# Batch 0's first product in six single PSUM banks, batch 1's exps moved ahead, and the activation tables loaded by hand, in an attention and feed-forward kernel

## The chip, the cores and the metric

The kernel runs on one core of one Trainium2 chip. The metric is the device time of one execution in microseconds (us); lower is better. Times inside an execution are counted from the start of the profile's span.

## What is computed

For 8 batches, 8 heads, 576 tokens of 64 dimensions, 32 packed queries p per head, all in float32:

```python
p_packed = sm_attn(p, k, v)              # softmax attention of the 32 packed queries over the tokens
out      = sm_attn(q, p_packed, p_packed) # the tokens attend to the 32 packed results
x = out.transpose(0, 2, 1, 3).reshape(8 * 576, 512)
h = x @ w_in                             # 512 -> 2048
g = h * np.cos(h)
return g @ w_out                         # 2048 -> 512
```

## The kernel before

All matrix work is in bfloat16 with float32 sums in PSUM. Batches go one after another through stages; within a stage the steps of the next batch's attention are laid between the matmuls of the current one. The order on every engine is the order of the program text (`tc.manual_schedule()`); the framework only adds the semaphores. Engines are PE (matmul), ACT (ScalarE), DVE (`V`, VectorE), POOL (`G`, GpSimd, which also issues the loads of k, q, v and the weights) and SP (which issues DMA transposes and the stores of the output).

The steps of a batch b, with the names that the profile shows:

- `load`: k, q, v come through POOL's DMA queue, cast to bf16 (`kbf`, `qbf`, `vbf`). `permute_v` copies v to `vp` (on POOL, batch 0 on DVE).
- k and q are transposed to `kT`, `qT`, either by `xbar` (a DMA transpose on SP's queue) or by `pe_T` (24 PE transposes in three groups, each evacuated from PSUM by ACT or DVE).
- `s1`: scores of p against k in two PSUM tiles, and their Exp on ACT (`a`, with row sums). `recips`: reciprocals of the sums on DVE (`r`, `rs`). `a` is transposed to `a1T` by `a1_xbar` (SP) or by PE (`a1_pe`, `a1_one`).
- `pp`: the packed result, 24 small matmuls of `vp` by `a1T`, copied to `ppT`. `ppw(b, n)`: its product with a quarter of w_in, copied to `PPW`, so that h can be formed from attention weights without forming x.
- `s2`: scores of q against the packed keys, Exp on ACT (`a2u`). `sums2`: sums over the packed tokens by a matmul with ones, and Ln on ACT (`lns`). `normalise`: Exp of minus that on ACT, and on DVE the product (`a2n`).
- `h_mm(b, fc)` for 16 slices fc of 128 hidden channels: h in PSUM by four matmuls of 288 columns (L250), cosine as Sin of h + pi/2 on ACT (`cosT`, L254), product on DVE (`gT`, L257). After fc 7 and 15 POOL copies the last 64 tokens to `joint`, which holds those of two batches.
- the output: for chunks of 128 tokens, 16 matmuls of `gT` by w_out (L303) into a bank `ot`, copied to `osb` by DVE and ACT in turn, stored by SP. These matmuls are the filler: `set_filler(b)` opens batch b's (64, or 80 where a chunk of `joint` is included), `fill(n)` issues n of them. The last chunk of all has a function of its own (L289).

PSUM has eight banks: three pairs (`psa()`, pool psA, used in turn) and two single ones (`bank()`, tag `ot`). Exp and Ln come from one activation table, Sin from another; before the change Exp's is loaded by hand (L354, L431, L454, L489) and Sin's by the compiler, at the first Sin (L254).

The stages: the head (loads, batch 0's attention, batch 1's s1); h(0), with the rest of PPW(0), `pp(1)` and q1's transposes in between; from `s2(1)` batch 1's attention and h(1) with batch 0's output as filler (`slot(1)` is the loop of h(1)); the same for stage 2 with `s1(2)`, `s1(3)`, `pp(2)`, h(2) and batch 1's output; a loop for stages 3 to 7; the output of batch 7.

POOL's `gate` copies read one element of a transposed tile, so that POOL's later loads are not issued before that transpose is done.

Of the kernel before, what the change touches and what calls it, by code (L numbers as in the profile page):

```python
# [8 lines left out]
FP32 = mybir.dt.float32  # L9
# [6 lines left out]
def kernel(  # L16
# [20 lines left out]
    EXP_SET = "natural_log_exp_and_others"  # L37

# [11 lines left out]
    A = ctx.enter_context(tc.tile_pool(name="psA", bufs=3, space=PSUM))  # L50
    O = ctx.enter_context(tc.tile_pool(name="psO", bufs=2, space=PSUM))

    ctx.enter_context(tc.manual_schedule())
# [24 lines left out]
    def psa(dt=FP32):  # L78
        return A.tile([128, 2, 512 if dt == FP32 else 1024], dt, name="psA", tag="A")

# [13 lines left out]
    def pe_T(n, b, engs=(V, V, V), groups=(0, 1, 2), own=False):  # L94
# [4 lines left out]
        for i in groups:  # L99
            ps = bank(BF16) if own else psa(BF16)[:, 0, :]  # L100
# [53 lines left out]
    def a1_pe(b, ys=(0, 1), own=False):  # L154
# [3 lines left out]
        for y in ys:  # L158
            ps = bank(BF16) if own else psa(BF16)[:, 0, :]
# [105 lines left out]
    n_out = [0]  # L265
# [29 lines left out]
    def out_gen(b):  # L295
        groups = [(0, 1), (2,), (3,)] if b == 0 else [(c,) for c in range(n_chunks(b))]
        for grp in groups:
            pss = {c: O.tile([128, DM], FP32, name="ot", tag="ot") for c in grp}
            for f0 in range(0, NFC, 4):
                for c in grp:  # L300
                    for fc in range(f0, f0 + 4):
# [41 lines left out]
    nc.sync.dma_start(out=p_raw[:, 0:2, :], in_=p_rows[:, 0:2, :])  # L343
# [5 lines left out]
    G.dma_start(out=p_raw[:, 2:4, :], in_=p_rows[:, 2:4, :])  # L349
# [12 lines left out]
    dup_p(0, 2, V)  # L362
    pack_p(0, 1)
# [186 lines left out]
```

## Time and profile before

| | |
|---|---|
| time, median of 3 runs | 254.32 us (254.19 to 255.27) |
| span of the profiled execution, first to last instruction | 252.3 us |
| granted TensorE clock, mean | 0.997 |
| PE, DVE, ACT, POOL busy | 92%, 65%, 68%, 23% |
| head, 0 to 22.7 us | first h matmul at 22.73 |
| h(0), 22.7 to 38.5 us | 15.8 us |
| stage 1, 38.5 to 63.9 us | 25.4 us |
| stage 2, 63.9 to 98.4 us | 34.5 us |
| stages 3, 4, 5, 6 | 25.5, 28.4, 26.1, 29.0 us |
| stage 7 and the last output | 21.9 and 23.0 us |

The profiled execution has no time of its own beside its span; it lies 2.0 us under the median of the timed runs, which counts what lies before the first and after the last instruction too. A line of the timeline gives start, length, engine, source line, operation, output and inputs, shapes and count, and in brackets how long the engine sat idle before it and what ended that. A PE line's length contains the pipeline's tail; two starts give the pace.

### The profile page before, as it was taken

To read this page: it belongs to the slowest core of one execution; us is meant where nothing else is said; L and a number is where in the kernel's file an instruction comes from. 1 tells how busy PE (TensorE), PEld (TensorE's weight loads), DVE (VectorE), ACT (ScalarE), POOL (GpSimd) and SP (SyncE) were. 2 spreads that over 40 slices of the span, in tenths; PEclk is the share of its full clock that TensorE was granted. 3 is DMA by queue.
4 is the path that set the end of the run, shared out by engine and by line. 5 is a ranking of instruction groups with operands and counts; after the bars stand their busy time and mean duration, and the time that the engine had idled before them with its cause. 6 is when DMAs were issued, how large, how long until landed. Compare 5 with 4: busy or idle time off the path is not lost.

```text
span 252.3 us, 4989 instructions
## 1 busy us (share of the span) xinstructions
PE 233.3 (92%) x1981; PEld 130.7 (52%) x2014; DVE 163.0 (65%) x245; ACT 170.5 (68%) x285; POOL 58.4 (23%) x71
## 2 busy tenths in 40 slices
PE   8786888999969999999999998999899999999993
PEld 3453463566435554465446553565356554665452
DVE  2548996789376977477847675479556874876110
ACT  2366888857558788878886667887877585873000
POOL 8442604200362243104313105020500000000000
PEclk9999999999999999999999999999999999999998
DMA  6999999999999989999999994979471112112133
GB/s 91 202 211 205 205 207 226 200 186 149 191 208 198 176 175 212 220 204 164 225 173 181 180 182 99 175 141 196 97 144 44 42 44 70 36 34 62 50 83 83
DMA packets 65270, 37.67 MB, mean 149 GB/s; under 512 B 37872, under 2 KB 60656, under 8 KB 65248
## 3 DMA queue, kind: packets, MB, share of 16 engines
q0 software_dynamic: 23184, 18.81, 48.8%
q1 hardware_dynamic: 41904, 18.42, 36.8%
q8 instruction: 15, 0.25, 0.4%
q10 hardware_dynamic: 160, 0.13, 0.2%
q14 instruction: 7, 0.06, 0.1%
HBM read 37.22 MB, written 9.44 MB: 185 GB/s over the span
## 4 chain that ended last, share of the span: by engine, by line
PE 74%; DVE 8%; ACT 7%; DMA 5%; issue 2%; POOL 2%; DVEq 0%; POOLq 0%; ACTq 0%
PE ot L303 42%; PE psA L250 22%; DMA w_in_bf<-in_moe_w_in_dram 5%; DVE gT L257 5%; PE psA L201 3%; ACT cosT L254 3%; PE psA L177 2%; PE psA L227 1%; PE ot L289 1%; ACT a2u L219 1%; ACT L489 1%; DVE rs L147 1%; PE psA L128 1%; DVE osb L76 1%; DVE PPW L76 1%
## 5 line engine op out<-in xcount | busy, mean ns | idle before, releaser
L303 PE MATMUL ot<-w_out_bf,gT 128*128 128x512 bf16 x483 | 126.9, 380 | 2.1 <-issue 1.3
L257 DVE TENSOR_TENSOR gT<-psA,cosT 128x576 bf16<-128x576 f32 x128 | 94.1, 754 | 31.1 <-ACT cosT L254 30.0
L254 ACT ACTIVATE cosT<-psA 128x576 bf16<-128x576 f32 x128 | 82.7, 652 | 29.8 <-PE psA L250 28.1
L250 PE MATMUL psA<-a2n,PPW 128*128 128x288 bf16 x512 | 84.0, 286 | 2.5 <-DVE PPW L76 1.0
L303 PEld LDWEIGHTS <-gT 128*128 128x128 bf16 x512 | 48.0, 98 | 42.6 <-issue 6.1
L250 PEld LDWEIGHTS <-PPW 128*128 128x128 bf16 x512 | 49.1, 98 | 36.5 <-issue 3.8
L76 DVE CAST PPW<-psA 128x1024 bf16<-128x1024 f32 (+1 forms) x23 | 25.8, 1128 | 12.1 <-PE psA L201 12.1
L261 POOL COPY joint<-gT 128x512 bf16<-128x512 bf16 x16 | 9.8, 614 | 88.7 <-DVE gT L257 88.7
L76 DVE COPY osb<-ot 128x512 f32<-128x512 f32 (+1 forms) x19 | 12.8, 671 | 16.9 <-PE ot L303 13.8
L74 ACT COPY osb<-ot 128x512 f32<-128x512 f32 (+1 forms) x18 | 10.3, 571 | 18.7 <-PE ot L303 14.1
L76 POOL COPY vp<-vbf 96x3072 bf16<-96x3072 bf16 x7 | 19.2, 2750 | 1.6 <-DMA vbf<-in_v_dram 1.6
L237 DVE SCALAR_TENSOR_TENSOR a2n<-a2u,r,lns 128x576 bf16<-128x576 bf16 x16 | 12.4, 813 | 9.6 <-ACT lns L235 9.6
L229 ACT ACTIVATE lns<-psA 128x576 f32<-128x576 f32 x16 | 10.3, 651 | 5.7 <-PE psA L227 5.3
L137 ACT ACTIVATE a<-psA 128x576 bf16<-128x576 f32 x16 | 10.2, 648 | 5.0 <-PE psA L128 5.0
L303 PE MATMUL ot<-w_out_bf,joint 128*128 128x512 bf16 x46 | 12.4, 380 | 0.1
L201 PE MATMUL psA<-w_in_bf,ppT 64*32 64x512 bf16 x224 | 10.4, 381 | 1.5 <-DVE gT L257 1.1
L219 ACT ACTIVATE a2u<-psA,rs 128x576 bf16<-128x576 f32 x16 | 11.0, 736 | 1.2 <-PE psA L128 1.1
L254 ACT ACT_TABLE_LOAD x8 | 10.3, 1283 | 0.1
L74 ACT CAST ppT<-psA 64x128 bf16<-64x128 f32 x24 | 6.2, 259 | 6.1 <-PE psA L103 2.9
L235 ACT ACTIVATE lns<-lns 128x576 f32<-128x576 f32 x16 | 10.0, 678 | 0.0
L341 PE MATMUL ot<-wz 128*128 128x512 bf16 x24 | 8.1, 472 | 1.5 <-DVE wz L353 1.2
L74 ACT CAST PPW<-psA 128x1024 bf16<-128x1024 f32 (+1 forms) x9 | 7.2, 826 | 2.6 <-PE psA L201 2.6
(71 smaller groups left out, 143.4 us busy)
## 6 DMA issues: line engine op xcount, KB each, us to landing
kbf<-in_k_dram POOLq DMA_DIRECT2D x8, 576.0 KB, 12.2
vbf<-in_v_dram POOLq DMA_DIRECT2D x8, 576.0 KB, 7.4
qbf<-in_q_dram POOLq DMA_DIRECT2D x8, 576.0 KB, 9.6
out_dram<-osb SPq DMA_DIRECT2D x24, 192.0 KB, 2.6
out_dram<-osb SPq DMA_DIRECT2D x22, 128.0 KB, 2.4
w_in_bf<-in_moe_w_in_dram POOLq DMA_DIRECT2D x4, 512.0 KB, 16.5
w_out_bf<-in_moe_w_out_dram POOLq DMA_DIRECT2D x4, 512.0 KB, 20.9
out_dram<-osb SPq DMA_DIRECT2D x26, 64.0 KB, 2.1
```

Of the source, the lines that this page charges most:

```text
L74: ACT.copy(out=out, in_=in_)
L76: eng.tensor_copy(out=out, in_=in_)
L137: ACT.activation(out=a1[b % 2][:, y, :, 0:TP].rearrange("p (e m) x -> p e m x", e=2), in_=ps[y][:, :, 0:HS].rearrange("p e (m x) -> p e m ...
L201: nc.tensor.matmul(ps[y][32 * x:32 * x + 32, :], ppT[b % 2][r, 2 * x + y, :], w_in_bf[r, x, n * 512:(n + 1) * 512], start=True, stop=True)
L219: ACT.activation(out=a2u[b][:, y].rearrange("p (e x) -> p e x", e=2), in_=ps[y][:, :, 0:HS], func=AF.Exp, scale=rs1[b][:, y:y + 1])
L229: ACT.activation(out=lns[b][:, y].rearrange("p (e x) -> p e x", e=2), in_=ps[:, :, 0:HS], func=AF.Ln)
L235: ACT.activation(out=lns[b][:, y], in_=lns[b][:, y], func=AF.Exp, scale=-1.0)
L237: V.scalar_tensor_tensor(out=a2n[b][:, y], in0=a2u[b][:, y], scalar=r1[b][:, y:y + 1], in1=lns[b][:, y], op0=ALU.mult, op1=ALU.mult)
L250: nc.tensor.matmul(ps[:, e, 0:HS], PPW[b][:, y, fc * 128:(fc + 1) * 128], a2n[b][:, y, e * HS:(e + 1) * HS], start=(y == 0), stop=(y == 1))
L254: ACT.activation(out=csv, in_=ps[:, :, 0:HS], func=AF.Sin, bias=PI_HALF)
L257: V.tensor_tensor(out=gT[b][:, fc, :].rearrange("p (e x) -> p e x", e=2), in0=ps[:, :, 0:HS], in1=csv, op=ALU.mult)
L303: nc.tensor.matmul(pss[c], w, w_out_bf[:, fc, :], start=(fc == 0), stop=(fc == NFC - 1))
```

## The change

- h(0) no longer uses `h_mm` but `h_one`: 512 tokens per slice in one bank, with the three pairs of psA closed and six single banks (psH) opened in their place for the time of h(0) (`banks(0)`, `banks(3)`). Two matmuls of 512 columns, a Sin and a product on 512. The last 64 tokens of all 16 slices follow at once in `h_rest(0)`, during h(1): 32 matmuls of 64 columns into one pair, one Sin and one product of 1024 columns, straight into `joint`.
- In the head p is loaded for two batches in one DMA on SP; k1's transposes go to the two `ot` banks between batch 0's sums; `s1(1)` comes right after `normalise(0)`, then Sin's table, then `ppw(0, 0)` whole, `a1_one(1)` and `recips(1)`.
- q1's transposes come after h(0) in single banks; batch 0's filler starts at `s2(1)`, with 18 matmuls before h(1) (4 were in h(0), 8 and 14 before h(1)).
- v2 is loaded ahead of q2 and k3; `permute_v(2)` and v3's load move into h(1); k2 is transposed by PE in h(1) (fc 7, 8, 9), q2 and k3 by SP from there; `load("k", 4)` follows `load("q", 3)`.
- `s1(3)`, `a1_xbar(3)` and `recips(3)` move from ahead of `pp(2)` to behind `normalise(2)`, which on SP is behind the transposes of q3 and k4; `permute_v(3)` stands ahead of the gate on k4.
- Both tables are loaded by hand: Sin's right behind the Exps, Exp's right behind the last Sin, ahead of the leftover filler. `osb` is copied by DVE between the Exps and by ACT during h (from h(1) on), no longer in turn.

```diff
--- before.py
+++ after.py
@@ -35,6 +35,7 @@
     EXP_SET = "natural_log_exp_and_others"
+    SIN_SET = "trig_and_small"
 
     const = ctx.enter_context(tc.tile_pool(name="const", bufs=1))
     bf_pool = ctx.enter_context(tc.tile_pool(name="bf", bufs=1))
@@ -47,10 +48,19 @@
     cos_pool = ctx.enter_context(tc.tile_pool(name="cos", bufs=3))
     o_pool = ctx.enter_context(tc.tile_pool(name="o", bufs=4))
     small = ctx.enter_context(tc.tile_pool(name="small", bufs=3))
-    A = ctx.enter_context(tc.tile_pool(name="psA", bufs=3, space=PSUM))
     O = ctx.enter_context(tc.tile_pool(name="psO", bufs=2, space=PSUM))
-
     ctx.enter_context(tc.manual_schedule())
+    psum = {"stack": ctx.enter_context(ExitStack())}
+
+    def banks(pairs):
+
+        psum["stack"].close()
+        if pairs:
+            psum["A"] = psum["stack"].enter_context(tc.tile_pool(name="psA", bufs=pairs, space=PSUM))
+        if pairs < 3:
+            psum["H"] = psum["stack"].enter_context(tc.tile_pool(name="psH", bufs=6 - 2 * pairs, space=PSUM))
+
+    banks(3)
     V, ACT, G = nc.vector, nc.scalar, nc.gpsimd
 
     w_in_bf = const.tile([128, 4, DF], BF16, name="w_in_bf")
@@ -76,7 +86,7 @@
             eng.tensor_copy(out=out, in_=in_)
 
     def psa(dt=FP32):
-        return A.tile([128, 2, 512 if dt == FP32 else 1024], dt, name="psA", tag="A")
+        return psum["A"].tile([128, 2, 512 if dt == FP32 else 1024], dt, name="psA", tag="A")
 
     def load(n, b):
         bf[n, b] = bf_pool.tile([TP, H, C * D], BF16, name=n + "bf", tag=n + "bf", bufs=2 if n == "k" else 1)
@@ -91,13 +101,16 @@
         t = xT[n, b] = att_pool.tile([128, H * 3, TP], BF16, name=n + "T", tag=n + "T", bufs=2 if n == "k" else 1)
         nc.sync.dma_start_transpose(out=t, in_=bf[n, b].rearrange("p h x -> p (h x)"))
 
-    def pe_T(n, b, engs=(V, V, V), groups=(0, 1, 2), own=False):
+    def one(dt=FP32):
+        return psum["H"].tile([128, 512 if dt == FP32 else 1024], dt, name="psH", tag="H")
+
+    def pe_T(n, b, engs=(V, V, V), groups=(0, 1, 2), own=None):
         if 0 in groups:
             xT[n, b] = att_pool.tile([128, H * 3, TP], BF16, name=n + "T", tag=n + "T", bufs=2 if n == "k" else 1)
         t = xT[n, b]
         flat = bf[n, b].rearrange("p h x -> p (h x)")
         for i in groups:
-            ps = bank(BF16) if own else psa(BF16)[:, 0, :]
+            ps = own(BF16) if own else psa(BF16)[:, 0, :]
             for j in range(8):
                 o = 8 * i + j
                 nc.tensor.transpose(ps[:, j * TP:(j + 1) * TP], flat[:, o * 128:(o + 1) * 128],
...
@@ -241,9 +254,7 @@
 
     def h_mm(b, fc):
         if fc == 0:
-            gT[b] = g_pool.tile([128, NFC, S], BF16, name="gT", tag="gT")
-            if b % 2 == 0:
-                joint[b // 2] = j_pool.tile([128, NFC, 128], BF16, name="joint", tag="joint")
+            g_tile(b)
         ps = psa()
         for y in range(2):
             for e in range(2):
@@ -262,7 +273,39 @@
                               in_=gT[b][:, fc - 7:fc + 1, 512:576])
         return rest
 
-    n_out = [0]
+    def g_tile(b):
+        gT[b] = g_pool.tile([128, NFC, S], BF16, name="gT", tag="gT")
+        if b % 2 == 0:
+            joint[b // 2] = j_pool.tile([128, NFC, 128], BF16, name="joint", tag="joint")
+
+    def h_one(b, fc):
+
+        if fc == 0:
+            g_tile(b)
+        ps = one()
+        for y in range(2):
+            nc.tensor.matmul(ps, PPW[b][:, y, fc * 128:(fc + 1) * 128], a2n[b][:, y, 0:512],
+                             start=(y == 0), stop=(y == 1))
+        cs = cos_pool.tile([128, 512], BF16, name="cosT")
+        ACT.activation(out=cs, in_=ps, func=AF.Sin, bias=PI_HALF)
+        V.tensor_tensor(out=gT[b][:, fc, 0:512], in0=ps, in1=cs, op=ALU.mult)
+
+    def h_rest(b):
+
+        t = psa()
+        for fc in range(NFC):
+            for y in range(2):
+                nc.tensor.matmul(t[:, fc // 8, (fc % 8) * 64:(fc % 8) * 64 + 64],
+                                 PPW[b][:, y, fc * 128:(fc + 1) * 128], a2n[b][:, y, 512:576],
+                                 start=(y == 0), stop=(y == 1))
+        cs = cos_pool.tile([128, 2, 512], BF16, name="cosR", bufs=1)
+        ACT.activation(out=cs, in_=t, func=AF.Sin, bias=PI_HALF)
+        j0 = (b % 2) * 64
+        V.tensor_tensor(out=joint[b // 2][:, :, j0:j0 + 64],
+                        in0=t.rearrange("p a (f x) -> p (a f) x", x=64),
+                        in1=cs.rearrange("p a (f x) -> p (a f) x", x=64), op=ALU.mult)
+
+    osb_eng = [V]
 
     def pieces_of(b, c):
         ob = out[b * S:(b + 1) * S, :].rearrange("(p c) d -> c p d", c=C)
@@ -304,8 +347,7 @@
                                          start=(fc == 0), stop=(fc == NFC - 1))
                         if fc == NFC - 1:
                             osb = o_pool.tile([128, DM], FP32, name="osb")
-                            copy((V, ACT)[n_out[0] % 2], osb, pss[c])
-                            n_out[0] += 1
+                            copy(osb_eng[0], osb, pss[c])
                             for a, z, rows in pieces_of(b, c):
                                 nc.sync.dma_start(out=rows, in_=osb[a:z, :])
                         yield
@@ -340,13 +382,12 @@
         for _ in range(n):
             nc.tensor.matmul(wps, wz[:, 0:128], wz, start=True, stop=True)
 
-    nc.sync.dma_start(out=p_raw[:, 0:2, :], in_=p_rows[:, 0:2, :])
+    nc.sync.dma_start(out=p_raw[:, 0:4, :], in_=p_rows[:, 0:4, :])
     load("k", 0)
     load("v", 0)
     make_identity(nc, ident)
     load("q", 0)
     load("k", 1)
-    G.dma_start(out=p_raw[:, 2:4, :], in_=p_rows[:, 2:4, :])
     for n in range(3):
         load_w_in(n)
     wz = const.tile([128, 512], BF16, name="wz")
@@ -359,8 +400,8 @@
         V.memset(t[:, :, :, TP:128], 0.0)
 
     warm(7)
-    dup_p(0, 2, V)
-    pack_p(0, 1)
+    dup_p(0, 4, V)
+    pack_p(0, 2)
     warm(9)
     pe_T("k", 0, (V, ACT, V))
     s1(0)
@@ -377,35 +418,50 @@
     for n in range(4):
         load_w_out(n)
     G.dma_start(out=p_raw[:, 4:, :], in_=p_rows[:, 4:, :])
-    s2(0)
-    warm(3)
-    dup_p(2, 4, V)
-    sums2(0, 0)
-    sums2(0, 1)
-    pe_T("k", 1, (V, V, V))
-    pack_p(1, 2, bank(BF16))
-    warm(2)
-    cut_ppw, rest_ppw = ppw(0, 0, V, own=True, later=True, cuts=((0, 128), (128, 512)))
-    normalise(0)
-    cut_ppw()
-    s1(1)
-    a1_one(1)
-    rest_ppw()
-    recips(1)
     load("k", 2)
     permute_v(1)
+    s2(0)
+    pe_T("k", 1, (V, V, V), (0,), own=bank)
+    sums2(0, 0)
+    pe_T("k", 1, (V, V, V), (1,), own=bank)
+    sums2(0, 1)
+    pe_T("k", 1, (V, V, V), (2,), own=bank)
+    warm(2)
+    normalise(0)
+    s1(1)
+    ACT.preload_act_table_set(SIN_SET)
+    cut_ppw, rest_ppw = ppw(0, 0, V, own=True, later=True, cuts=((0, 128), (128, 512)))
+    cut_ppw()
+    rest_ppw()
+    a1_one(1)
+    recips(1)
+    banks(0)
     for fc in range(NFC):
-        h_mm(0, fc)()
-        if fc in (1, 5, 8):
+        h_one(0, fc)
+        if fc in (1, 5, 9):
             ppw(0, 1 + fc // 4, (ACT, V), own=True)
-        if fc == 10:
+        if fc == 13:
             pp(1, own=True, engs=(ACT, ACT))
-        if fc in (11, 12, 13):
-            pe_T("q", 1, (V, ACT, V), (fc - 11,), own=True)
-        if fc == 13:
-            set_filler(0)
-        if fc >= 14:
-            fill(2)
+    ACT.preload_act_table_set(EXP_SET)
+    pe_T("q", 1, (ACT, V, V), own=one)
+    load("v", 2)
+    load("q", 2)
+    load("k", 3)
+    dup_p(4, 2 * B, G)
+    banks(3)
+    set_filler(0)
+    s2(1)
+    ppw(1, 0, V)
+    fill(2)
+    sums2(1, 0)
+    fill(2)
+    sums2(1, 1)
+    fill(4)
+    ppw(1, 1, V)
+    fill(4)
+    normalise(1)
+    ACT.preload_act_table_set(SIN_SET)
+    fill(6)
 
     def slot(s, hooks, keep=0, heavy={}):
         left = filler[1] - keep
@@ -426,43 +482,35 @@
         ppw(b, n + 1, eng)
 
     def tk(n, b, i):
-        return lambda: pe_T(n, b, (V, V, V), (i,))
-
+        return lambda: pe_T(n, b, (ACT, V, ACT), (i,))
+
+    def late():
+        permute_v(2)
+        load("v", 3)
+
+    def cross(n, b):
+        return lambda: xbar(n, b)
+
+    osb_eng[0] = ACT
+    slot(1, [(1, lambda: pw2(1, 2, (ACT, V))), (2, late), (4, lambda: h_rest(0)),
+             (6, lambda: pack_p(2, 5)), (7, tk("k", 2, 0)), (8, tk("k", 2, 1)), (9, tk("k", 2, 2)),
+             (9, cross("q", 2)), (10, lambda: pack_p(5, B)), (12, cross("k", 3))], 4)
     ACT.preload_act_table_set(EXP_SET)
-    s2(1)
-    ppw(1, 0, V)
-    load("q", 2)
-    load("k", 3)
-    load("v", 2)
-    dup_p(4, 2 * B, G)
-    fill(8)
-    sums2(1, 0)
-    sums2(1, 1)
-    xbar("k", 2)
-    xbar("q", 2)
-    xbar("k", 3)
+    osb_eng[0] = V
     G.tensor_copy(out=gate, in_=xT["k", 3][0:1, 0, 0:1])
     load("q", 3)
-    ppw(1, 1, V)
-    normalise(1)
-    fill(14)
-    slot(1, [(3, lambda: pw2(1, 2, (ACT, V))), (6, lambda: pack_p(2, 5)), (8, lambda: pack_p(5, B)),
-             (8, lambda: (permute_v(2), load("v", 3), load("k", 4)))], 4)
+    load("k", 4)
 
     fill(1000)
     set_filler(1)
-    ACT.preload_act_table_set(EXP_SET)
     s1(2)
     fill(10)
     a1_pe(2, (0,))
     fill(3)
     a1_pe(2, (1,))
     recips(2)
-    fill(3)
-    s1(3)
+    fill(6)
     pp(2)
-    a1_xbar(3)
-    recips(3)
     fill(6)
     s2(2)
     ppw(2, 0, V)
@@ -473,20 +521,25 @@
     ppw(2, 1, V)
     sums2(2, 1)
     normalise(2)
-    G.tensor_copy(out=gate, in_=a2n[2][0:1, 1, 0:1])
+    s1(3)
+    ACT.preload_act_table_set(SIN_SET)
+    a1_xbar(3)
+    recips(3)
+    fill(4)
     permute_v(3)
-    fill(8)
     G.tensor_copy(out=gate, in_=xT["k", 4][0:1, 0, 0:1])
     for n, b in (("v", 4), ("q", 4), ("k", 5)):
         load(n, b)
-    fill(8)
+    fill(9)
+    osb_eng[0] = ACT
     slot(2, [(3, lambda: pw2(2, 2, (ACT, V))), (7, lambda: pp(3, engs=(ACT, ACT))), (11, lambda: pw2(3))], 5, {11: 3})
 
     for s in range(3, B):
         nxt = s + 1 < B
+        ACT.preload_act_table_set(EXP_SET)
+        osb_eng[0] = V
         fill(1000)
         set_filler(s - 1)
-        ACT.preload_act_table_set(EXP_SET)
         if nxt:
             permute_v(s + 1)
         s2(s)
@@ -509,7 +562,9 @@
         fill(5)
         sums2(s, 1)
         normalise(s)
+        ACT.preload_act_table_set(SIN_SET)
         fill(13)
+        osb_eng[0] = ACT
         for n, b in (("v", s + 2), ("q", s + 2), ("k", s + 3)):
             if b < B:
                 load(n, b)
```

More of the change, by code (lines that the diff above doesn't have):

```diff
@@ L152, in a1_xbar, with a1_pe @@
                                     in_=a1[b % 2].rearrange("p a c x -> p (a c x)"))
-    def a1_pe(b, ys=(0, 1), own=False):
+    def a1_pe(b, ys=(0, 1)):
         if 0 in ys:
@@ L158, in a1_pe @@
         for y in ys:
-            ps = bank(BF16) if own else psa(BF16)[:, 0, :]
+            ps = psa(BF16)[:, 0, :]
             for c in range(C):
```

## Prediction

> **What bounds the kernel now.** I read the page's busy shares, then the windows cut at each stage's first scores, then the timeline around every PE gap.
>
> ```profile
> PE 233.3 (92%) x1981; PEld 130.7 (52%) x2014; DVE 163.0 (65%) x245; ACT 170.5 (68%) x285; POOL 58.4 (23%) x71
> 22.70:38.50 15.80, 13.31 (x143) 8.05 (x141) 14.55 (x25) 12.82 (x25) 5.62 (x5) 1.00 1.27 205
> 38.50:63.90 25.40, 24.14 (x190) 13.70 (x192) 19.94 (x28) 18.35 (x28) 4.45 (x6) 1.00 1.30 190
> 63.90:98.40 34.50, 31.30 (x305) 17.05 (x311) 23.82 (x34) 25.36 (x45) 12.41 (x14) 1.00 1.11 192
> 123.90:152.30 28.40, 28.08 (x233) 15.53 (x236) 19.02 (x27) 20.30 (x35) 6.50 (x8) 1.00 1.02 176
> ```
>
> The columns after the length are busy PE, PEld, DVE, ACT, POOL, the granted clock, DMA. From 38.5 us PE sets the time (28.08 of 28.40 in stage 4): there, added matmuls cost their full length and only PE waits can be gained. In h(0) DVE is the bound (14.55 of 15.80).
>
> ```profile
> 22.93 0.55 DVE L76 COPY a1T<-psA 96x768 bf16<-96x768 bf16 x1 [0.59 <-PE psA L169]
> 26.88 2.93 DVE L257 TENSOR_TENSOR gT<-psA,cosT 128x576 bf16<-128x576 f32 x4
> 33.18 1.07 ACT L74 CAST ppT<-ot 64x128 bf16<-64x128 f32 x4
> 39.68 0.41 PE L201 MATMUL psA<-w_in_bf,ppT 64*32 64x512 bf16 x8 [0.61 <-DVE gT L257]
> 40.14 1.37 ACT L219 ACTIVATE a2u<-psA,rs 128x576 bf16<-128x576 f32 x2
> 42.82 1.22 DVE L76 CAST PPW<-psA 128x1024 bf16<-128x1024 f32 x1 [1.44 <-PE psA L201]
> 44.00 1.55 DVE L237 SCALAR_TENSOR_TENSOR a2n<-a2u,r,lns 128x576 bf16<-128x576 bf16 x2
> ```
>
> The head, in order: DVE waits for the second half of a1T's transposes; four multiplies back to back (0.725 us each); ppT copies that hold up Sin; PE waiting for the last multiply; the cast and a2n ahead of h(1).
>
> ```profile
> 68.64 2.75 POOL L76 COPY vp<-vbf 96x3072 bf16<-96x3072 bf16 x1
> 68.90 2.52 DVE L147 TENSOR_SCALAR rs<-r 128x2 f32<-128x2 f32 x1
> 71.44 0.87 PE L177 MATMUL psA<-a1T,vp 96*128 96x64 bf16 x24 [2.23 <-DVE rs L147]
> 72.93 4.99 SPq L151 DMA_TRANSPOSE a1T<-a  x1
> 75.83 1.22 DVE L76 CAST PPW<-psA 128x1024 bf16<-128x1024 f32 x1 [0.34 <-PE psA L201]
> 152.41 0.58 ACT L74 COPY osb<-ot 128x512 f32<-128x512 f32 x1 [1.08 <-PE ot L303]
> 153.01 1.28 ACT L489 ACT_TABLE_LOAD   x1
> 154.31 1.37 ACT L219 ACTIVATE a2u<-psA,rs 128x576 bf16<-128x576 f32 x2
> 155.10 0.44 PE L128 MATMUL psA<-kT,P 64*32 64x288 bf16 x16 [0.31 <-ACT a2u L219]
> ```
>
> Two places lose PE time later: pp(2) waits for vp(2), permuted late (DVE's 0.17 us rs is stuck beside it); in stages 5 and 6 an osb copy on ACT delays the Exp table, then a2u, then PE.
>
> **Unit prices.** One w_out matmul: 16 from 75.95 to h(2) at 79.41, 0.216. Eight transposes, 34.30 to 34.64: 0.34. pp's 24 matmuls of 64 columns, 87.39 to 88.09: 0.029 each. [...]
>
> **Before h(0).** k1's transposes fit between the sums; the Ln and normalising Exps stay at 17.16 to 19.55. P's copy (0.28) no longer precedes a2n, which goes from 19.70 to 19.0 and ends at 20.55. w_in's first quarter (landed 19.63, its product at 20.24) stays hidden; p_raw in one DMA on SP spares POOL one 0.73 us issue; what queues behind it are w_in's loads, which nothing waits for. k2's load and permute_v(1) keep their places on POOL. Exps of batch 1 at 19.6, Sin's table ready at 22.2, not 23.1. But DVE then has: first PPW cut 0.48, the rest 1.01 (22.04), a1T 0.55 (22.59), a wait of 0.59 for the second transposes as now, a1T 0.55 (23.73). The six single banks lie where the three pairs lay. No row shows how a reopened pool waits: 0 if bank by bank, 0.73 if for the old pool's last reader. I take 0.73, as both banks of the last pair are read until then. So the first h matmul is at 23.8 (now 22.73) and the first multiply at 25.0 (now 24.60).
>
> **h(0).** DVE: 16 x 0.66 plus three PPW halves x 0.65 = 12.5; the ppT copies on ACT delay the next Sin, which costs DVE 0.63 now (34.96) and about 0.9 with Sin less far ahead. 25.0 + 12.5 + 0.9: the last multiply ends at 38.4 (now 39.62). q1's copies now come behind: 2 x 0.55 on DVE, 39.5; on ACT the Exp table (1.28) and 0.80 end at 39.6. So s2(1) is at 39.6 (now 38.51) and its Exps at 40.0 (now 40.14): the shorter multiplies are given back. PE has its last transposes out by about 37.2 (h is up to six banks ahead of DVE) and idles 2.4 us before s2(1); the four w_out matmuls once in h(0) are gone.
>
> **To h(1).** Before the change 26 w_out matmuls (4 + 8 + 14) are done at h(1)'s start, 45.6; after it 18. From s2(1) PE needs 5.4 us to h(1): 18 x 0.216 and the scores, sums and two PPW products, 45.0. DVE is later: ppw(1,1) at 42.5, its cast 0.48 behind (42.34 to 42.82 now) for 1.22, to 44.2; a2n 1.55, to 45.75. The old order has 14 matmuls over these, the new one ten, so h(1)'s second half waits 0.55. Same start in effect, eight matmuls behind: 8 x 0.216 = +1.73.
>
> **Slot 1.** The remainder, 32 matmuls of 64 columns: 32 x 0.029 = +0.93 on PE (up to 32 x 0.056 = 1.8 if paced like the a transposes, 6 in 0.33); its Sin (1.0) and multiply (1.2) fit beside PE's 1.05 us per step. k2's 24 transposes: +1.02, in exchange for SP's 7.04 us DMA transpose, which bound nothing. PSUM waits: now 0.7; then 0.3 at the earlier PPW pair and 0.3 at k2's tiles, whose ACT copies take 0.80 (0 to 0.7). So s1(2) moves from 63.9 to 67.5: 1.73 + 0.93 + 1.02 - 0.1 = +3.6.
>
> **Stage 2.** v2 is issued at 31.5, behind permute_v(1), and lands near 51, permuted in slot 1: pp(2)'s 2.5 us gap (s1(3) at 68.9 to 71.44) goes. What is late next: s1(3), now right behind sums2. Its second tile is the buffer of ppw(2,1), freed by the cast ending 1.7 us after that product's start: PE waits 1.0, with 13 w_out matmuls queued behind (0 if another buffer is free). Its Exps (1.37) and the Sin table end about when h(2) needs them. On POOL permute_v(3) now stands ahead of the gate on k4, at about 69 to 72, clear of batch 2's rs. Net -1.5.
>
> **Stages 3 to 7.** Loading the Exp table ahead of the leftover matmuls, with osb on DVE, removes 2 x 0.75 in stages 5 and 6 (155.10 and 155.73, and their likes); osb on ACT in the slots may cost stages 3 and 7 what it costs stage 5, 0.28, less 0.35 lost to osb on DVE in stage 3: +0.2. Explicit Sin tables sit where the loads already run, right behind the Exps. Net -1.3. [...]
>
> **Sum.** +1.73 +0.93 +1.02 -0.1 -1.5 -1.3 = +0.8. The span is 252.3; the median of the runs is 2.0 above it (start, end and another execution), so the change is laid on the median: 255.1. About 0.5% (1.3 us) can be told from no change.
>
> **Rivals.** *Faster:* the PSUM buffers don't wait as I charge: pool 0.73, s1(3) 1.0, the PPW pair 0.3, k2 0.3, in all 2.3, so +0.8 becomes -1.5: 252.8. For it: nothing in the trace shows these waits. Against: PE waits on psA readers at every stage (39.68, 155.10). Chance 0.22.
> *Slower:* SP's order. a1's transpose of batch 3 now stands behind those of q3 and k4, and k4's behind its load. I get k4's transpose at 80 to 83.5, a1T landed near 87, pp(3) due 8 us into the slot, 89.5. With durations as now (q 6.87, a 4.99; k4's load took 12) it lands near 92: pp(3) stalls 2.5, +3.3 in all: 257.6. It decides once k4's transpose starts after 84. For: the busy DMA, 1.11. Against: v3's load is long done by then. Chance 0.17.
> *Clock:* PE idle before s2(1) drops the granted clock. The first seven warm-up matmuls took 3.17 us, nine right after 2.52; the first pace is half the second, and four us of it cost 2, +2.8 in all: 257.1. Against: 2.5 us idle at 68.9 kept it at 1.00. Chance 0.07. [...]
> *Not what it says:* the explicit loads come on top of automatic ones, 1.28 each on ACT, hidden but once, at the end of h(0): +1.3 on the 0.8, 256.4. Chance 0.04.
>
> **Numbers.** My forecast has 0.50, of which 0.12 is over +1.3 (the remainder at 1.8, longer copy waits). Faster by over 0.5%: 0.16 from the first rival, its other 0.06 counting as same. Slower: 0.12 + 0.17 + 0.07 + 0.02 = 0.38; same 0.46. The range goes from the faster case less 0.5 (k2's and the slots' remaining losses), 252.3, to the SP case, 257.6; the forecast alone reaches from 254.2 to 256.2.
>
> **What would show it.** First h matmul near 23.8, last multiply near 38.4, s2(1) near 39.6; s1(2) near 67.5; no gap before pp(2), one of 1 us at s1(3); no ACT wait in stages 5 and 6. Wrong, if s1(2) is before 66 (h(0) or slot 1 mis-sized), pp(3) waits, or the clock leaves 1.00 before the end.

## The result, and the profile after

| | before | after |
|---|---|---|
| time, median (runs) | 254.25 us (253.78 to 255.27, 4 runs) | 257.39 us (256.41 to 258.23, 4 runs) |
| span of the profiled execution | 252.3 us | 256.3 us (its own time 258.04) |
| granted TensorE clock, mean | 0.997 | 0.987 |

The ratio after to before is 1.0123 (95%: 1.0086 to 1.016): slower by 1.2%. The forecast was 255.1 us, with 257.1 for the Clock rival. Ratios, here and below, leave out runs more than 1.5% above the fastest of their kernel; medians and ranges are of all runs.

The page's busy row and clock row (tenths of full speed in 40 slices) of the changed kernel:

```profile
PE 235.0 (92%) x2000; PEld 130.0 (51%) x2035; DVE 161.4 (63%) x239; ACT 174.3 (68%) x293; POOL 56.3 (22%) x67
PEclk9999797999999999999999999999999999999999
```

Its windows, cut at the same events as before (first h matmul, first scores of each stage), with the same columns:

```profile
24.30:40.20 15.90, 11.96 (x105) 5.11 (x107) 12.96 (x23) 13.33 (x25) 6.86 (x6) 0.89 1.26 206
40.20:71.00 30.80, 28.74 (x243) 16.20 (x247) 19.90 (x26) 21.04 (x32) 5.72 (x5) 0.94 1.08 179
71.00:104.40 33.40, 31.80 (x300) 17.37 (x304) 23.84 (x35) 23.94 (x44) 8.16 (x10) 1.00 1.05 181
104.40:256.20 151.80, 145.90 (x1152) 81.58 (x1172) 92.05 (x124) 104.97 (x174) 24.13 (x26) 1.00 0.63 118
```

The column behind the five engines' busy times is the granted clock. h(0) is 15.9 us long (15.8 before); stage 1 grew from 25.4 to 30.8; stage 2 fell from 34.5 to 33.4, stages 3 to 7 from 153.9 to 151.8. The new thing is the clock: 0.89 in h(0), 0.94 in stage 1, two sevens in the clock row. The same view, cut finer around the two places:

```profile
21.40:24.80 3.40, 1.13 (x12) 0.76 (x10) 2.49 (x8) 1.45 (x3) 0.74 (x1) 1.00 1.28 205
24.80:28.20 3.40, 3.18 (x15) 0.87 (x15) 2.30 (x4) 2.46 (x5) 1.46 (x2) 0.50 1.28 209
38.45:41.86 3.41, 1.11 (x27) 0.66 (x29) 2.23 (x4) 2.61 (x4) 1.06 (x2) 1.00 1.24 229
41.86:45.27 3.41, 3.41 (x18) 1.18 (x16) 0.34 (x1) 2.73 (x5) 0.00 (x0) 0.50 1.23 218
```

Twice PE was busy for only 1.1 of 3.4 us, and twice the next 3.41 us were granted half the clock. In the second of these PE is busy all the time and does the work of half that time: four w_out matmuls take 1.91 us there, and 1.03 in e1 below, at 1.00.

The timeline's lines that answer to those of the head and of the way to h(1):

```profile
24.29 1.40 PE L287 MATMUL psH<-a2n,PPW 128*128 128x512 bf16 x4 [0.64 <-DVE a1T L86]
25.59 1.45 DVE L291 TENSOR_TENSOR gT<-psH,cosT 128x512 bf16<-128x512 f32 x2 [1.08 <-ACT cosT L290]
35.84 1.08 ACT L84 CAST ppT<-ot 64x128 bf16<-64x128 f32 x4
37.57 1.29 DVE L291 TENSOR_TENSOR gT<-psH,cosT 128x512 bf16<-128x512 f32 x2 [0.95 <-ACT cosT L290]
40.19 0.44 PE L141 MATMUL psA<-qT,ppT 64*32 64x288 bf16 x16 [2.50 <-ACT qT L84]
43.38 1.91 PE L346 MATMUL ot<-w_out_bf,gT 128*128 128x512 bf16 x4
45.72 1.23 DVE L86 CAST PPW<-psA 128x1024 bf16<-128x1024 f32 x1 [3.52 <-PE psA L214]
46.86 1.84 DVE L250 SCALAR_TENSOR_TENSOR a2n<-a2u,r,lns 128x576 bf16<-128x576 bf16 x2
48.75 0.41 PE L261 MATMUL psA<-a2n,PPW 128*128 128x288 bf16 x2 [0.32 <-DVE a2n L250]
```

To s2(1) each point is where the forecast had it plus 0.5 to 0.6 us. Then four w_out matmuls take 1.91 us, ppw(1,1) behind them is late, DVE sits idle for 3.52 us for it, and the second half of h(1) begins at 48.75 where the forecast had 45.8. The same two points in e1 below, where the clock holds (the four matmuls, and the second half of h(1)):

```profile
41.83 1.03 PE L346 MATMUL ot<-w_out_bf,gT 128*128 128x512 bf16 x4
46.00 0.41 PE L261 MATMUL psA<-a2n,PPW 128*128 128x288 bf16 x2 [0.29 <-DVE a2n L250]
```

The timeline of stage 2, and of the start of stage 5, where the Exp table now stands ahead of the leftover matmuls:

```profile
74.61 2.76 POOL L86 COPY vp<-vbf 96x3072 bf16<-96x3072 bf16 x1
75.74 1.66 DVE L160 TENSOR_SCALAR rs<-r 128x2 f32<-128x2 f32 x1
76.18 0.86 PE L190 MATMUL psA<-a1T,vp 96*128 96x64 bf16 x24
78.91 0.60 PE L141 MATMUL psA<-qT,ppT 64*32 64x288 bf16 x15 [0.35 <-ACT ppT L84]
80.98 1.34 ACT L242 ACTIVATE lns<-psA 128x576 f32<-128x576 f32 x2 [0.32 <-PE psA L240]
81.36 1.23 DVE L86 CAST PPW<-psA 128x1024 bf16<-128x1024 f32 x1 [0.33 <-PE psA L214]
82.37 0.32 PE L141 MATMUL psA<-kT,P 64*32 64x288 bf16 x8 [0.38 <-ACT lns L242]
157.01 1.28 ACT L539 ACT_TABLE_LOAD   x1
158.35 1.37 ACT L232 ACTIVATE a2u<-psA,rs 128x576 bf16<-128x576 f32 x2
```

pp(2) waits for nothing, the table load and the Exp have no idle time ahead of them; but rs, of two elements per partition, takes 1.66 us beside POOL's copy, and s1(3) waits, as foreseen. (A bracket holds the idle time of the whole engine, and the modelled ends of PE's matmuls hide a part of a wait. Counted from the w_out matmul ahead to the one behind, and against e15 below, where neither waits, s2(2) with the PPW product behind it lost 1.03 us and s1(3) 0.69.)

### The profile page after: what moved, and what is told of

Its sections match the earlier page's. It is cut to its first block, busy times and chain, and to the rows that moved or that the text cites. A ratio compares the mean times of both kernels' runs of the same rounds, so it can differ in the third digit from the quotient of the medians.

```text
span 256.3 us, 5021 instructions
## 1 busy us (share of the span) xinstructions
PE 235.0 (92%) x2000; PEld 130.0 (51%) x2035; DVE 161.4 (63%) x239; ACT 174.3 (68%) x293; POOL 56.3 (22%) x67
## 4 chain that ended last, share of the span: by engine, by line
PE 76%; DVE 9%; ACT 6%; DMA 4%; issue 3%; POOL 1%; DVEq 0%; ACTq 0%; POOLq 0%
PE ot L346 43%; PE psA L261 21%; DMA qbf<-in_q_dram 4%; DVE gT L291 2%; DVE PPW L86 2%; PE psA L141 2%; PE psA L214 2%; PE psA L240 2%; DVE gT L268 1%; PE psA L190 1%; PE ot L332 1%; DVE a2n L250 1%; ACT cosT L265 1%; PE psH L287 1%; ACT a2u L232 1%
## 5 line engine op out<-in xcount | busy, mean ns | idle before, releaser
L346 PE MATMUL ot<-w_out_bf,gT 128*128 128x512 bf16 x482 | 128.4, 383 | 2.0 <-issue 0.9
L268 DVE TENSOR_TENSOR gT<-psA,cosT 128x576 bf16<-128x576 f32 x112 | 83.3, 757 | 34.5 <-ACT cosT L265 33.5
L265 ACT ACTIVATE cosT<-psA 128x576 bf16<-128x576 f32 x112 | 72.5, 652 | 26.2 <-PE psA L261 24.6
L261 PE MATMUL psA<-a2n,PPW 128*128 128x288 bf16 x448 | 73.4, 286 | 1.2 <-DVE PPW L86 0.4
L261 PEld LDWEIGHTS <-PPW 128*128 128x128 bf16 x448 | 43.7, 98 | 31.2 <-issue 2.0
L86 DVE COPY osb<-ot 128x512 f32<-128x512 f32 (+1 forms) x14 | 9.4, 672 | 21.3 <-PE ot L332 17.4
L84 ACT COPY osb<-ot 128x512 f32<-128x512 f32 (+1 forms) x23 | 13.2, 574 | 13.5 <-PE ot L346 12.4
L291 DVE TENSOR_TENSOR gT<-psH,cosT 128x512 bf16<-128x512 f32 x16 | 10.2, 685 | 2.5 <-ACT cosT L290 2.4
L290 ACT ACTIVATE cosT<-psH 128x512 bf16<-128x512 f32 x16 | 8.9, 604 | 3.8 <-PE psH L287 3.4
L287 PE MATMUL psH<-a2n,PPW 128*128 128x512 bf16 x30 | 9.2, 426 | 2.1 <-DVE PPW L86 1.2
```

The costliest lines, as they stand in the source:

```text
L84: ACT.copy(out=out, in_=in_)
L86: eng.tensor_copy(out=out, in_=in_)
L261: nc.tensor.matmul(ps[:, e, 0:HS], PPW[b][:, y, fc * 128:(fc + 1) * 128], a2n[b][:, y, e * HS:(e + 1) * HS], start=(y == 0), stop=(y == 1))
L265: ACT.activation(out=csv, in_=ps[:, :, 0:HS], func=AF.Sin, bias=PI_HALF)
L268: V.tensor_tensor(out=gT[b][:, fc, :].rearrange("p (e x) -> p e x", e=2), in0=ps[:, :, 0:HS], in1=csv, op=ALU.mult)
L287: nc.tensor.matmul(ps, PPW[b][:, y, fc * 128:(fc + 1) * 128], a2n[b][:, y, 0:512], start=(y == 0), stop=(y == 1))
```

## The experiments

All ratios below are to the kernel before, run beside.

### The clock: PE kept busy in one idle place, in the other, in both

**e1_busy_before_s2**, the changed kernel, ten matmuls that nobody uses between q1's transposes and s2(1):

```diff
     pe_T("q", 1, (ACT, V, V), own=one)
+    warm(10)
```

> The changed kernel with ten dummy matmuls (on zeros, into an output bank) behind q1's transposes, in PE's 2.67 us of idling before s2(1); everything else as it is. Clock theory: the half-clock stretch at 41.9 to 45.3 is the answer to that idling and slows 18 w_out matmuls and ppw(1,1) with all that hangs on it; it goes, s2(1) to h(1)'s second half takes 6.2 us and not 8.6, the time falls by 2.0 to 2.5 from 257.4 to about 255.1, mean clock 0.990 or more. Order theory (the length from s2(1) to h(1) comes from the order of cast, sums and a2n, whatever the clock): time stays at 257.4 within 0.5. [...]

256.41 us (255.49 to 257.05), ratio 1.0094 (1.0059 to 1.0129). The profiled execution had no stretch at half clock: s2(1) at 39.38, the second half of h(1) at 46.00 (6.62 behind it, against 8.56 in the changed kernel), span 253.7. The median fell by 1.0 us and not by the 2.0 to 2.5 expected: two of the four runs still show a drop in their mean clock (0.990 and 0.993; 256.55 and 257.05 us), and two none (1.000; 255.49 and 256.28).

**e2_busy_in_head**, seven such matmuls between the two halves of `a1_one(1)`, where PE waits 1.63 us for the copy of the first:

```diff
             copy(V, t[0:TP, y].rearrange("p c x -> p (c x)"), ps[0:TP, y, 0:C * 128])
+            if y == 0:
+                busy = psa()[:, 0, :]
+                for _ in range(7):
+                    nc.tensor.matmul(busy, wz[:, 0:128], wz, start=True, stop=True)
```

> The changed kernel with seven dummy matmuls between the two halves of a1_one(1), where PE idles 1.8 us; nothing else. Clock theory in its plain form (a half-clock stretch of 3.4 us costs 1.7 us): the stretch at 24.8 to 28.2 goes and 1.7 us with it, 255.7. My reading of the traces: h(0) is bound by DVE, so that stretch costs nothing: it goes, the mean clock rises by 0.007, and the time stays at 257.4 within 0.5.

257.33 us (255.29 to 257.56), ratio 1.0115 (1.0066 to 1.0164). The head's stretch is gone, that behind s2(1) is still there (39.42 to 42.84, behind 3.41 us with 1.18 busy). The median stays, as the second reading expected, but the traces don't bear that reading out: from the first h matmul to s2(1) it took 15.17 us (15.90 in the changed kernel), so the head's stretch cost 0.7. The medians hide it because they mix executions: two runs of the changed kernel have a mean clock of 0.987 (258.04 and 258.23 us), two 0.991 and 0.992 (256.74 and 256.41); here three runs are at 0.991 or 0.992 (257.32 to 257.56), and the one at 1.000 took 255.29.

**e3_busy_both**, both edits:

> Both dummy groups. Clock theory: no half-clock stretch before the end, mean clock 0.996 or more, time near the forecast of 255.1, and every execution alike (spread under 0.5 us, where the changed kernel has 256.4 to 258.2). If the stretch in the head costs nothing, as the first group alone (e1) within 0.4. Order theory: 257.4.

255.47 us (255.21 to 255.85, 6 runs), ratio 1.0057 (1.0036 to 1.0077). The windows of its trace at the same two places, and the one behind the second:

```profile
21.40:24.80 3.40, 2.63 (x17) 1.27 (x15) 2.39 (x8) 1.34 (x2) 0.74 (x1) 1.00 1.27 204
38.45:41.86 3.41, 2.51 (x35) 1.25 (x35) 1.73 (x3) 2.60 (x5) 0.23 (x1) 1.00 1.24 222
41.86:45.27 3.41, 3.41 (x23) 1.35 (x22) 2.02 (x3) 3.22 (x5) 0.00 (x0) 1.00 1.25 220
```

Seventeen matmuls that compute nothing make the kernel 1.9 us faster (257.39 to 255.47; 1.7 by the ratios), because the clock stays at 1.00 (0.997 to 1.000 in all six runs); and the runs lie within 0.6 us of each other instead of 1.8 (under 0.5 was expected). What is left, 1.2 us over the kernel before (254.28), is the forecast's +0.8 with some more.

### p in two DMAs again

**e4_p_split**, the changed kernel with the old loading of p (batch 0's by SP, batch 1's by POOL):

```diff
-    nc.sync.dma_start(out=p_raw[:, 0:4, :], in_=p_rows[:, 0:4, :])
+    nc.sync.dma_start(out=p_raw[:, 0:2, :], in_=p_rows[:, 0:2, :])
...
+    G.dma_start(out=p_raw[:, 2:4, :], in_=p_rows[:, 2:4, :])
```

> The changed kernel with p loaded as before: the first half on SP, the second on POOL behind k1, its cast and transposes behind s2(0). If the doubled first load holds up k0 (landed at 8.12, before at 7.37) and with it the whole head, k0 lands near 7.4, the first h matmul is 0.5 to 0.75 earlier (24.29 now), and so is s2(1); time 0.5 to 0.75 less, 256.8. If w_in or DVE sets the head anyway, s2(1) stays at 40.2 and the time at 257.4.

257.18 us (256.27 to 257.99), ratio 1.0126 (1.0089 to 1.0163). k0 landed at 7.30 us (8.12 in the changed kernel) and s2(0) started at 14.78 (15.59), so the head gains 0.8; none of it reaches s2(1), which came at 40.40: in this execution the clock was halved from 21.90 to 28.72, two stretches in a row.

### Parts of the change alone, on the kernel before

**e5_table_ahead**:

```diff
         fill(1000)
         set_filler(s - 1)
-        ACT.preload_act_table_set(EXP_SET)
```

with the load ahead of `fill(1000)`, and `osb_eng` as in the change (DVE there, ACT in the slots of stages 3 to 7).

> The kernel before, with one part of the change: in stages 3 to 7 Exp's table is loaded ahead of the leftover matmuls, and osb is copied by DVE there and by ACT during the slots. Theory (the forecast's step): the ACT waits of 1.08 and the PE waits of 0.31 and 0.4 at 155 us, and their likes in stage 6, go, 2 x 0.75, less 0.2 for osb on ACT in the slots: 1.3 us less, 253.0 where the kernel before has 254.3. Rival: PE waits there for PSUM pairs and not for the table, so the waits only change their releaser: 254.3.

254.13 us (251.33 to 256.53, 10 runs), ratio 0.9932 (0.9881 to 0.9982): faster by 0.7%. The waits of PE at the start of stages 5 and 6 are gone in its trace. The times fall in two groups, three runs at 251.3 to 251.7, six at 253.8 to 254.7, one at 256.5. The mean granted clock of the three is 0.997 to 1.000, that of all others 0.993 or less; one stretch of 3.4 us at half clock is worth 0.007. The profiled one (254.12) is of the second group; its windows show where:

```profile
68.90:72.30 3.40, 1.29 (x42) 0.95 (x42) 3.12 (x4) 1.37 (x4) 3.10 (x2) 1.00 0.90 135
72.30:75.70 3.40, 3.40 (x33) 0.93 (x29) 0.91 (x4) 0.91 (x3) 1.59 (x3) 0.50 1.19 257
```

This is the gap ahead of pp(2), which the kernel before has too (the two programs are the same up to there). There, in the profiled execution, it fell across the edge of two windows:

```profile
66.62:70.03 3.41, 2.53 (x34) 1.36 (x34) 2.31 (x4) 1.50 (x6) 2.89 (x4) 1.00 0.74 145
70.03:73.44 3.41, 1.94 (x29) 1.21 (x30) 2.89 (x6) 0.88 (x4) 3.11 (x4) 1.00 1.14 195
```

Each window keeps 1.9 us busy or more, and the clock stays at 1.00. The same idle time cost nothing more there, and 1.5 us more here (stage 2 is 36.0 us long, for 34.5); where the windows' edges lie is the difference that the two traces show. The 31 runs of the kernel before that stand beside this one have both kinds: the eleven with a mean clock of 0.996 or more took 253.7 to 255.0 us, the twenty with 0.993 or less 253.5 to 259.8. So a stretch can also cost nothing; where it fell in those runs is not known.

**e6_v2_early**, the kernel before with v2 first and permuted at once:

```diff
+    load("v", 2)
     load("q", 2)
     load("k", 3)
-    load("v", 2)
     dup_p(4, 2 * B, G)
+    permute_v(2)
+    load("v", 3)
```

> The kernel before, with v2 loaded ahead of q2 and k3, and permute_v(2) and v3's load right behind dup_p on POOL. Theory: pp(2)'s gap of 2.5 us at 68.9 to 71.4 goes whole: 251.8. Rival: the same wait comes back as a later one, because q2 and k3 land some 3 us later, their transposes on SP end later, and s2(2) or s1(3) waits for them: 253 to 254.3, with the new wait visible between 65 and 76 us.

255.97 us (255.46 to 261.38, 10 runs), ratio 1.0039 (0.9999 to 1.0079): the gain that was expected is not there. pp(2)'s gap is gone, and in the timeline two new ones stand ahead of it (the last line is of SP's queue):

```profile
66.39 0.44 PE L128 MATMUL psA<-kT,P 64*32 64x288 bf16 x16 [1.80 <-DMA kT<-kbf]
72.00 0.44 PE L128 MATMUL psA<-kT,P 64*32 64x288 bf16 x16 [0.94 <-DMA kT<-kbf]
72.37 0.87 PE L177 MATMUL psA<-a1T,vp 96*128 96x64 bf16 x24
55.71 10.96 SPq L92 DMA_TRANSPOSE qT<-qbf  x1
```

k2's transpose, issued at 48.54 as before, landed 17.8 us later (13.2 in the kernel before, and due at 63.9), with v3's load, issued at 54.44, now beside it; q2's took 10.96 us on SP instead of 5.83. So k2 by PE, which I had booked as 1.02 us for something that "bound nothing", is what makes the earlier loads pay (e16 below, without this transpose on SP, has neither wait).

**e7_both_on_before**, both of these:

> The kernel before with both of these parts (tables and osb as in e5_table_ahead, v2 early as in e6_v2_early) and nothing of the rest. They lie in different stages, so they should add: 254.3 - 1.3 - 2.5 = 250.5. If it is within 0.3 of the sum of the two measured gains, the remainder of the change (h(0) in single banks, the head's new order, slot 1) is what loses all that they win.

254.34 us (252.22 to 257.26, 10 runs), ratio 0.9979 (0.9939 to 1.0019). Not 250.5: in its trace s1(2) waits 2.14 us for k2's transpose, and pp(4) 2.04 for a1T of batch 4. The two measured parts (-0.68% and +0.39%) add to -0.29%, within its interval, so the times don't contradict adding; but one of the parts is no gain, and the wait of pp(4) stands in the trace of neither part.

### The changed kernel mended step by step

**e13_real_filler**, e3 with ten matmuls of batch 0's output in place of the ten idle ones:

```diff
     pe_T("q", 1, (ACT, V, V), own=one)
+    set_filler(0)
+    fill(10)
...
-    set_filler(0)
     s2(1)
```

> The changed kernel with the clock kept up: the seven idle-time matmuls in the head as in e3_busy_both, and ahead of s2(1) ten matmuls of batch 0's output in place of ten that do nothing. Theory: the ten are work taken out of stage 1 (10 x 0.216 = 2.2 us) and put into PE's idle time, so 255.5 (e3_busy_both) becomes 253.3, s2(1) stays at 39.4, and the clock stays at 1.00. Rival: h(1)'s start is set by DVE (cast and a2n of batch 1), so less filler ahead of it is no loss, and the output copies that come with the filler delay the copies of q1's transposes: 254.5 to 255.5.

255.38 us (254.53 to 257.67, 10 runs), ratio 1.0022 (0.9983 to 1.0061): within the rival's numbers, but not for its reason. In the profiled execution (256.85) s2(2) did come 1.7 us earlier than in e3 (73.83, 75.49). Then SP's queue, and PE behind it, in the timeline:

```profile
83.20 3.12 SPq L102 DMA_TRANSPOSE kT<-kbf  x1
86.42 1.47 SPq L164 DMA_TRANSPOSE a1T<-a  x1
90.26 1.10 PE L194 MATMUL psA<-a1T,vp 96*128 96x64 bf16 x24 [1.90 <-DMA a1T<-a]
```

pp(3) now waits for a1T, and behind that gap the clock is halved (90.70 to 94.11). It is the forecast's slower rival, SP's order, hidden in the changed kernel only because that was late: there a1T landed at 90.92 and pp(3) was due at 93.42.

**e14_a1_first**, e13 with the order on SP changed:

```diff
     ppw(2, 0, V)
-    xbar("q", 3)
-    xbar("k", 4)
...
     a1_xbar(3)
+    xbar("q", 3)
+    xbar("k", 4)
```

> The kernel of e13_real_filler with one thing moved: on SP the transpose of a1T of batch 3 is issued ahead of those of q3 and k4 instead of behind them. Theory (SP's order, the forecast's slower rival, comes true once the head is earlier): pp(3) waited 1.90 us at 88.3 for a1T, which started when k4's transpose was through (88.18) and landed at 90.12; with a1T first it lands near 85 and the wait goes, 255.3 becomes 253.4, also because the clock's drop behind that wait (90.7 to 94.1) goes. Rival: a1's transpose then runs beside the loads of q3 and k4, takes 8 us or more (12.0 in the kernel before) and still lands after pp(3) is due: no change, 254.5 to 255.5.

253.23 us (253.07 to 257.1, 10 runs), ratio 0.9969 (0.994 to 0.9998). pp(3) starts at 88.23 without a wait, and no stretch is at half clock before the end. As the theory had it (253.4).

**e15_all_mended**, e14 with p in two DMAs and six w_out matmuls moved ahead of s1(3):

```diff
+    fill(6)
     s1(3)
...
-    fill(4)
...
-    fill(9)
+    fill(7)
```

> The changed kernel with every loss that was found mended: the seven idle-time matmuls in the head, ten matmuls of batch 0's output ahead of s2(1), p in two DMAs, six w_out matmuls moved ahead of s1(3), a1T's transpose ahead of those of q3 and k4. Theory: 253.4 (e14_a1_first) less 0.6 for p and 0.4 for s1(3), 252.4. Rival: DVE's work between the two batches sets h(1)'s start, so p's gain is lost there: 253.

252.37 us (252.22 to 252.7, 5 runs), ratio 0.9912 (0.9879 to 0.9946). s1(3) waits for nothing, and stage 2, from its first scores to those of stage 3, is 32.14 us (32.59 in e14), the 0.4 expected. The profiled head came no earlier (s2(0) at 15.26, e14 15.32: k0 landed at 7.78 and 7.85), so a share for p is not shown by this pair, and the rest of the 0.9 us between the two medians is not explained.

### Without the single banks

**e16_no_single_banks**, the kernel before up to s2(1), the change's order behind it (without the remainder), and a1T first on SP:

```diff
+    load("v", 2)
     load("q", 2)
     load("k", 3)
-    load("v", 2)
...
-    xbar("k", 2)
-    xbar("q", 2)
-    xbar("k", 3)
...
+    slot(1, [(2, late), (3, lambda: pw2(1, 2, (ACT, V))), (6, lambda: pack_p(2, 5)),
+             (7, tk("k", 2, 0)), (8, tk("k", 2, 1)), (9, tk("k", 2, 2)), (9, cross("q", 2)),
+             (10, lambda: pack_p(5, B)), (12, cross("k", 3))], 4)
```

> The kernel before up to s2(1), so h(0) in the old form and no remainder in slot 1, followed by the change's order from there: v2 early, k2's transposes by PE in slot 1, s1(3) behind normalise(2), tables and osb as in the change, and a1T's transpose ahead of those of q3 and k4. Theory: the single banks and the new head cost, the rest pays: 254.4 + 1.0 (k2 on PE) + 0.1 - 1.3 (stage 2, as in the trace of the changed kernel) - 2.1 (stages 3 to 7) = 252.1, and because pp(2)'s gap is gone the clock has no place to drop, so the runs lie closer together than those of the kernel before. If k2's transposes are what made the v2 move pay, pp(2), s1(2) and s1(3) wait for no DMA, unlike in e6_v2_early. Rival: the loads, now issued in the same order with nothing earlier, land no later than before, and s1(3)'s wait for its PSUM tile takes what pp(2) gave: 254.

252.64 us (252.27 to 256.7, 10 runs), ratio 0.9917 (0.9877 to 0.9957): 0.5 above the theory's 252.1. k0 landed 0.43 later in the profiled execution than in the kernel before, which moves everything behind. The theory's terms fit less well than its sum: stage 1 grew by 2.0 us (1.1 expected), and stage 2 fell by 1.9 (1.3 expected). pp(2), s1(2) and s1(3) wait for no DMA, unlike in e6. That the clock would have no place to drop was wrong: three of the ten runs are at 0.990 to 0.992 and took 255.0 to 256.7 us; no trace shows where it fell in them. So this version, which never touches h(0), and the mended one with the single banks (0.9912) can't be told apart: both beat the kernel before and the changed one, and the banks are not what does it.

**e17_no_single_banks_s1**, e16 with the six matmuls ahead of s1(3) as in e15:

> The kernel of e16_no_single_banks, with six w_out matmuls moved ahead of s1(3), from behind it. Theory (the forecast's step that s1(3) waits for a PSUM tile that PPW's cast must leave): its wait of 0.39 and the second one behind it go, 252.6 becomes 252.1. Rival: Exps of batch 3 and Sin's table then end after h(2) is ready to start, so h(2) waits for Sin by as much: 252.6.

253.86 us (251.93 to 257.16, 8 runs), ratio 0.9927 (0.9881 to 0.9973): no gain shown over e16. Four runs are at 251.9 to 252.7, four at 255.0 to 257.2. The profiled one (255.94) is one of the four above; it shows one way to get there. s1(3)'s wait is gone in it. But in the timeline:

```profile
70.67 3.52 DVE L147 TENSOR_SCALAR rs<-r 128x2 f32<-128x2 f32 x1
71.40 2.76 POOL L76 COPY vp<-vbf 96x3072 bf16<-96x3072 bf16 x1
75.03 0.29 PE L128 MATMUL psA<-qT,ppT 64*32 64x288 bf16 x1 [1.76 <-DVE ppT L76]
```

and in the windows:

```profile
73.20:76.60 3.40, 1.26 (x26) 0.46 (x26) 2.08 (x5) 1.04 (x3) 0.95 (x1) 1.00 1.31 199
76.60:80.03 3.43, 3.43 (x17) 1.17 (x16) 1.92 (x2) 1.65 (x4) 0.00 (x0) 0.50 0.77 163
```

rs meets permute_v(3), ppT is late, PE idles, the clock drops. In e16's profiled execution rs ran from 71.12 to 71.29 and the copy began at 72.02: it passed by 0.7 us. The gate on a2n of batch 2 that kept permute_v(3) away before is one of the lines that the change removes. That this collision makes the upper four runs (mean clock 0.987 to 0.993) is a guess from one trace, not shown: one of the lower four is at 0.990 too; a version with that gate back was not run.

## Why the prediction was right and wrong

The time came inside the range, close to its upper edge; the likeliest case, no change, was wrong, and the case that came true was the one given 0.07. That the range holds it is partly luck: its upper edge was the SP case, which didn't happen.

**The step that failed: the clock.** I had the idle time right (2.4 us before s2(1) forecast, 2.50 measured), and the price of one stretch there too (2.0 forecast; from s2(1) to the second half of h(1) the changed kernel's trace is 1.94 longer than e1's). But two stretches came: by s2(1) that trace is already 0.81 later than e1's, 0.08 of it from ahead of the first h matmul and the rest from the head's stretch, and its span is 2.6 longer. What failed is the reason against it: "2.5 us idle at 68.9 kept it at 1.00". That was one execution with the windows' edges in a lucky place (1.94 us busy or more in each); e5, the same gap behind the same program, had 1.29 in one and lost its clock there. And I looked at one gap only: the head has waits of 1.63 and 0.64 us close together, and the clock fell behind those too. Part of that idle time is from my own sum: the wait of the a1T transposes and the 0.73 at the reopened banks. The windows that cost the clock were not empty: in the traces of these runs the 3.41 us ahead of a stretch had 1.1 to 1.8 us of PE busy. So an idle time well under 3.4 us can cost it: 2.50 us, and 1.63 with 0.64, did here.

**p in one DMA, "spares POOL one issue".** It costs: k0, which travels beside it, landed at 7.79 to 8.36 in the six traces with both batches' p in one DMA, and at 7.30 to 7.80 in the eight with it split, 0.5 later on average. I had looked at what queues behind on POOL, not at what travels beside it. No pair of runs shows what that is worth in the time: in e4's trace the gain went to the clock, and in e15's k0 landed as late as in e14's.

**h(0).** Two waits right: the first h matmul in the reopened banks waits for the last reader of the old pool (0.64 on PE, 0.73 charged), and the stall behind ppT is 0.95 (0.9 charged). From first multiply to the end of the last it took 13.3 us (13.4 forecast), but that holds the first half-clock stretch; in e1 it is 12.5, mostly because four multiplies take 2.48, 0.62 each. The 0.66 that the forecast charges for one was my estimate, and no run shows it; what they show is 0.73 on 576 columns in the kernel before (four in 2.93) and 0.62 on 512 in e1. q1's copies and the Exp table behind h(0) give back what the shorter multiplies won, as worked out.

**Slot 1.** One term right, k2's transposes with three times 0.34. The remainder's 32 matmuls take 1.15 from start to start (51.49 to 52.64 in e1), where 0.93 was charged. The PSUM waits were undersized, -0.1. In e1, from the second half of h(1) to s1(2), it took 22.27 us where the forecast has 67.5 - 45.8 = 21.7. The wait that I missed is that of p's transposes for the remainder's 1.23 us product on DVE: an h step of 0.49 took 0.97 there, so 0.48.

**Stage 2.** -1.1 for -1.5. The gap went. s1(3) lost 0.69 (1.0 charged), but not for the reason given: its second half started at 82.37, when the cast of ppw(2,1) had still 0.2 us to run; it came right behind the Ln on the sums, which ended at 82.32. Which buffer that is, the profile doesn't show. The step "permute_v(3) ... clear of batch 2's rs" was wrong: it ran from 74.61, not 69 to 72, met rs, and cost s2(2) and the product behind it 1.0.

**Stages 3 to 7.** -2.1 for -1.3: the two waits went as worked out, and the +0.2 for osb on ACT wasn't there; stage 3 gained 0.3 too, and the others 0.1 each (e5 alone shows stage by stage nearly the same as the whole change: stage 5 25.2 for 26.0 us, stage 6 28.35 for 29.1).

**SP's order** was a sound rival at the wrong time: not in the changed kernel, but in e13, where pp(3) waited 1.90 for it, and e14, which undoes it, is 2.15 us faster. The rival of the PSUM buffers that don't wait is false: both big waits are in the trace. No table is loaded twice: the traces of before and after have 16 loads of 1.28 us each.

With the clock held, e3: 255.47 us for a forecast of 255.1. That it is so close is luck too: in e3's trace s2(1) is 0.25 earlier than forecast, stage 1 then takes 1.0 and stage 2 0.3 longer, and stages 3 to 7 0.8 less.

## What to carry to other kernels

An idle gap of TensorE is priced by more than its length: add up PE's busy time over any 3.4 us around it, and where about half or less is left (the clock fell here behind 1.11 to 1.84 us busy of 3.41), count up to 2 us more with some chance (0.7, 1.5 and 1.9 in three places of these traces), which then shows as scatter between executions; work moved out of a stage should therefore leave some matmuls, useful ones if there are any, in its gaps. A part that gains alone in a trace may be paid for by another part of the same change (v2 early by k2 on PE), and a slack that a transfer has is slack only while what is ahead of it is late. When two engines' copies are reordered, look at the tiny instructions beside the long ones (rs, 0.17 us alone, took 1.58 to 3.52 beside POOL's copy).

## What the runs showed of the hardware

- Ahead of the end the clock falls to 0.50 for 3.413 us at a time (once for two of these in a row, in e4), and where these begin differs between executions: the two in the changed kernel's trace begin at 24.80 and 41.86, five times 3.413 apart, others at 22.87 (e6), 39.42 (e2) and 72.30 (e5), on no grid from the span's start that all share. In these traces it fell behind 3.41 us with 1.11 and 1.13 (the changed kernel), 1.18 (e2), 1.26 (e17), 1.29 (e5) and 1.51 us (e13) of PE busy, and in the head behind 1.76 (e4) and 1.84 (e6); it did not behind 1.62 (e6), 1.65 and 1.66 (e7), 1.70 and 1.80 (e1), 1.88 (e5) and 1.94 (the kernel before), nor, once, behind 1.41 (e4, 38.97 to 42.37). So busy time as the profile shows it is not all that decides; what else does is open.
- rs, a DVE instruction of 0.17 us in e16, ended with a POOL copy of 2.75 us in all eight traces where the two overlap in stage 2, 0.02 to 0.04 behind it: at 77.40 in the changed kernel and at 74.19 in e17, the copies at 77.37 and 74.16. In e17 rs began 0.73 before the copy, while POOL was issuing a load, and still ended behind it; in e16 it ran its 0.17 us during such an issue. What ties the two is not shown.
- k2's DMA transpose took 17.8 us to land in e6, with v3's load beside it, and 13.2 in the kernel before.
